# Plain float32 products for the first four head pairs, and weight groups spread over the steps of y

## The chip, the cores and the metric

The kernel runs on one core of a Trainium2 chip. The metric is the device time of one execution in microseconds, as the median of several runs; a profiled execution has its own time, which is given beside it. The core has five engines with a queue each: PE (TensorE, the matrix unit; its weight loads are listed as PEld), DVE (VectorE), ACT (ScalarE), POOL (GpSimd) and SP (SyncE, which here issues the DMAs). Each queue runs in order.

## The reference

Attention over 4 batches of 8 heads, 576 tokens of 64 numbers each, with a second, linear path through a memory; then two feed-forward layers over 2,304 tokens. The inputs are float32, or float64 words for some weights, and the result is wanted at nearly float32 precision.

```python
scores = scale * q @ k.T                 # causal, per head, 576 x 576
a = softmax(scores);  local = a @ v
q_p = where(q > 0, q, exp(q) - 1) + 1
mem_out = (q_p @ M_prev) / (q_p . z_prev + 1e-6)
attn = g * mem_out + (1 - g) * local     # g = sigmoid(beta), per head
x = attn as 2304 x 512
h = x @ w_in                             # 512 -> 2048
y = (s * relu(h)**2 + b) @ w_out         # 2048 -> 512
gate = sigmoid(y @ w_gate);  val = y @ w_val      # 512 -> 1536
out = (gate * val) @ w_out2              # 1536 -> 512
```

## The kernel before

**Products in parts.** PE multiplies operands of type float32r, a rounded float32, at one column after the other. To keep the precision an operand is split into a high part (the value rounded to float32r) and a low part (what is left, float32r again), and a product is made of three: high x high, low x high, high x low. The high part is usually a copy on ACT, the low part a subtraction on DVE or POOL. Weights come as 64-bit words and are first converted to float32 on ACT (L247) and DVE (L250, L253, L259); then ACT (L265) and POOL (L268) split them.

**Stages.** (1) Attention works on 16 jobs j, each a pair of heads of one batch, four to a batch. q, k and v are loaded (SP), q and k are transposed on PE (L413) and split; scores (L623, L649), maximum (DVE, L603), exponent (ACT, L665), scaling by the reciprocal sums (POOL, L681). The rows of P are transposed on PE in eight groups A0 to D1 (L750, GROUPS, 25 blocks of 128 x 128), copied as the high part by ACT (L773) and subtracted for the low part by DVE (L777). v is split on POOL (L587, L590) into 64 high and 64 low columns side by side, M_prev too (L401, L404), and phi(q), transposed, is split into FS by L421, L422 (ACT) and L426, L427 (DVE). `pv(win, e)` (L779) then makes, for head e and each of two windows of tokens (0 to 256, 256 to 576), one accumulator `acc` of 128 rows, the upper 64 for the products with high columns of v, the lower 64 for those with the low ones; every term over P takes two products (L803, L804), the term over M_prev one (L807). ACT copies the lower half into XB (L827) and DVE adds the upper half (L831).

(2) When a batch is done, x is split (ACT L888, POOL L892) and h = x @ w_in is made in 128 chunks of 12 products (L316) that run between the attention of the later batches; ACT applies relu and SP stores r.

(3) y runs in 96 steps, six token windows of 384 by 16 blocks of rows. A step loads r (`rr`), squares it (ACT L1025), scales it (DVE L1029), copies the high part `gh` (ACT L1035), subtracts for the low part `gl` (POOL L1040) and makes 12 products (PE L1054). In the same phase the 24 pieces of w_gate and w_val are converted, combined pair by pair into 12 groups (`plan_blocks`, sums in L1159) and stored in DRAM.

(4) z makes three pairs of token windows. For each pair, 12 groups of products (L1291) from the stored weight groups, added up by DVE (L1303), passed through a sigmoid or multiplied (POOL L1313) to `p`; then six out tiles, each of three groups of four blocks (`plan_out`): copy (ACT L1369), subtraction (DVE L1376), 12 products (L1387).

**Order.** No engine's order is written by hand. Every piece of work is a task with an engine, an assumed duration, an urgency (base plus offset from the dict TUNE), tiles read and written, and buffers taken. `Plan.order` simulates the engines, each time starting the ready task with the lowest urgency, and the instructions are emitted in the order found; semaphores follow from the tiles that instructions share, not from the plan. Buffers of a kind are handed out in the order in which the tasks are listed.

Of the kernel before, what the change touches and what calls it, by code (L numbers as in the profile page):

```python
# [30 lines left out]
}  # L31
ENG = {"split": "POOL"}
RR = 4
RAW2 = 4
RING = 5
SETS = 3


class Plan:
# [25 lines left out]
    def order(self):  # L65
# [34 lines left out]
        while len(out) < len(tasks):  # L100
            for eng in clock:
                if clock[eng] > now:
                    continue
                for n in ready.get(eng, []):
# [15 lines left out]
                    heapq.heappush(events, (end, n))  # L120
                    heapq.heappush(events, (clock[eng], -1))
# [6 lines left out]
            while events and events[0][0] <= now:  # L128
                _, n = heapq.heappop(events)
                if n < 0:  # L130
                    continue
                for x in tasks[n][5]:
                    touches[x] -= 1
                    if not touches[x] and x in self.made:
                        free[self.made[x][0]] += 1
                for m in users[n]:
                    waiting[m] -= 1
# [10 lines left out]
def attention_moe_kernel(  # L148
# [267 lines left out]
    def bank(nt):  # L416
        return "s" if nt <= 4 else "w"
# [6 lines left out]
    def stack_lo(t, ds):  # L424
# [10 lines left out]
        "raw2": RAW2, "f2": FB, "w2": 16, "rr": RR, "gh": 3, "gl": 3, "yacc": 2,  # L435
# [30 lines left out]
    def plan_prep(j):  # L466
# [90 lines left out]

        def f_hi():
# [14 lines left out]
            new=[(bank(nt), ("ft", j)), ("FS", ("FS", j, 0)), ("FS", ("FS", j, 1))], late=250)  # L573
        add(
# [18 lines left out]

        add("POOL", 950, lambda: prep_m(j), u + AT["m"], reads=[("mem", j)], new=[("mst", ("m", j))])
# [928 lines left out]
```

## Time and profile before

| | us |
|---|---|
| runs | 1143.1, 1136.14, 1135.06 (median 1136.14) |
| profiled execution | 1142.42 |
| its span, first to last instruction | 1140.6 |
| PE busy | 1056.0 (93%) |
| DVE busy | 786.0 (69%) |
| ACT busy | 647.3 (57%) |
| POOL busy | 619.2 (54%) |

The mean granted TensorE clock of the span is 0.975 of full speed. A busy PE is not a PE at its peak: products overlap, so a product's listed duration is longer than the distance to the next one's start. An engine that is idle off the chain that ends last costs nothing. The stages follow each other in time: attention alone to about 105 us, attention and h to about 405, h and y to about 507, y to about 706, z and out to the end.

### The profile page before, as it was taken

Reading aid. Unit: us, or ns where it says so; the run is one execution under the profiler, and the core shown is the slowest. Engines: PE = TensorE matmul, PEld = TensorE weight load, DVE = VectorE, ACT = ScalarE, POOL = GpSimd, SP = SyncE. Lnnn points to the kernel's source line nnn. Section 1 sums busy time; section 2 is a strip of 40 time slices with the busy share of each in tenths; the row PEclk is TensorE's granted clock in tenths of the full one; section 3 lists DMA queues with packets and bytes.
Section 4 is the critical chain, followed back from the end, with each engine's and each line's share of the span. In section 5 each row is a group of like instructions: output and inputs, shape, how many; then the busy total and the mean of one; then the engine's idle time right before and its main releaser. Section 6 shows DMA issues by size and latency. Waiting matters only on the chain.

```text
span 1140.6 us, 18761 instructions
## 1 busy us (share of the span) xinstructions
PE 1056.0 (93%) x6496; PEld 986.6 (86%) x6496; DVE 786.0 (69%) x1426; ACT 647.3 (57%) x1407; POOL 619.2 (54%) x598
## 2 busy tenths in 40 slices
PE   4776999999999989988789999999799998999998
PEld 3665999899999989988688999998689997899986
DVE  5999888777677527868999433999826667166631
ACT  4877777777777655545656544555425553245421
POOL 5657566744454335733665653999615775157710
PEclk9989899999999999988899999999999999999999
DMA  5333453333232157649588634545114330043100
GB/s 129 76 78 100 120 158 119 85 94 94 83 95 66 59 185 207 197 139 346 184 250 289 218 112 133 205 156 193 59 44 146 130 129 10 37 138 130 66 19 37
DMA packets 135598, 145.93 MB, mean 128 GB/s; under 512 B 68176, under 2 KB 123472, under 8 KB 135504
## 3 DMA queue, kind: packets, MB, share of 16 engines
q1 hardware_dynamic: 135504, 144.74, 40.5%
q8 instruction: 51, 0.84, 0.3%
q14 instruction: 43, 0.35, 0.1%
HBM read 106.96 MB, written 37.75 MB: 127 GB/s over the span
## 4 chain that ended last, share of the span: by engine, by line
PE 71%; DVE 15%; DMA 4%; issue 3%; POOL 3%; ACT 3%; SPq 0%; ACTq 0%; DVEq 0%; POOLq 0%
PE m L1291 19%; PE h L316 15%; PE o L1387 13%; PE y L1054 11%; PE sc L623 3%; PE acc L803 2%; PE acc L804 2%; DMA rr<-relu_scratch 1%; DVE wm L1159 1%; PE pt_B L750 1%; DVE rr L1029 1%; PE sc L649 1%; PE ft L413 1%; POOL p L1313 1%; DVE yt L1190 1%
## 5 line engine op out<-in xcount | busy, mean ns | idle before, releaser
L1291 PE MATMUL m<-yt,ws 128*128 128x384 f32 x1512 | 266.9, 336 | 6.5 <-POOL ws L1275 3.9
L1291 PEld LDWEIGHTS m<-yt,ws 128*128 128x128 f32 x1512 | 263.6, 189 | 9.1 <-POOL ws L1275 4.8
L316 PE MATMUL h<-x,w_in 128*128 128x256 f32 (+1 forms) x1536 | 233.6, 305 | 6.9 <-ACT r L326 6.9
L316 PEld LDWEIGHTS h<-x,w_in 128*128 128x128 f32 x1536 | 214.3, 194 | 13.1 <-ACT r L326 8.2
L1303 DVE TENSOR_TENSOR set<-m,set 128x384 f32<-128x384 f32 x252 | 134.2, 553 | 57.4 <-PE m L1291 55.3
L1275 POOL TENSOR_TENSOR ws<-wf,ws 128x512 fp32r<-128x512 f32 (+1 forms) x108 | 123.8, 1165 | 90.5 <-ACT ws L1267 90.4
L1054 PE MATMUL y<-gh,w_out 128*128 128x384 f32 x768 | 155.9, 344 | 17.8 <-ACT gh L1035 16.4
L1040 POOL TENSOR_TENSOR gl<-rr,gh 128x384 fp32r<-128x384 f32 x96 | 111.2, 1169 | 112.2 <-ACT gh L1035 83.9
L1387 PE MATMUL o<-w_out,ps 128*128 128x512 f32 x648 | 155.6, 401 | 8.8 <-DVE ps L1376 8.8
L1387 PEld LDWEIGHTS o<-w_out,ps 128*128 128x128 f32 x648 | 123.6, 191 | 39.7 <-DVE ps L1376 10.0
L1054 PEld LDWEIGHTS y<-gh,w_out 128*128 128x128 f32 x768 | 137.6, 193 | 22.4 <-ACT gh L1035 18.8
L1267 ACT CAST ws<-wf 128x512 fp32r<-128x512 f32 (+1 forms) x144 | 81.1, 568 | 94.2 <-PE m L1291 66.7
L1029 DVE TENSOR_SCALAR rr<-rr,sb_s,sb_b 128x384 f32<-128x384 f32 x96 | 62.5, 663 | 71.5 <-ACT rr L1025 69.2
L1313 POOL TENSOR_TENSOR p<-set,set 128x384 f32<-128x384 f32 x72 | 85.2, 1206 | 45.4 <-DVE set L1303 45.4
L681 POOL TENSOR_SCALAR P<-P,rs 128x384 f32<-128x384 f32 (+3 forms) x144 | 82.9, 599 | 42.0 <-DVE rs L673 24.2
L603 DVE CUSTOM_DVE_ANT_0 P<-sc,mask 128x384 f32<-128x384 f32 (+2 forms) x144 | 70.8, 515 | 34.7 <-PE sc L623 19.2
L665 ACT ACTIVATE P<-P,nm 128x384 f32<-128x384 f32 (+2 forms) x144 | 83.8, 583 | 7.4 <-DVE nm L603 6.7
L1054 PE MATMUL y<-gl,w_out 128*128 128x384 f32 x384 | 84.4, 341 | 1.1 <-POOL gl L1040 1.1
L326 ACT ACTIVATE r<-h 128x320 f32<-128x320 f32 (+1 forms) x128 | 52.2, 409 | 57.3 <-PE h L316 42.2
L1376 DVE TENSOR_TENSOR ps<-p,ps 128x512 fp32r<-128x512 f32 x54 | 47.1, 886 | 50.6 <-ACT ps L1369 50.2
L1025 ACT ACTIVATE rr<-rr 128x384 f32<-128x384 f32 x96 | 49.4, 524 | 50.9 <-DMA rr<-relu_scratch 48.8
L1054 PEld LDWEIGHTS y<-gl,w_out 128*128 128x128 f32 x384 | 69.5, 192 | 2.3 <-POOL gl L1040 2.3
(134 smaller groups left out, 1709.8 us busy)
## 6 DMA issues: line engine op xcount, KB each, us to landing
wf<-weight_scratch SPq DMA_DIRECT2D x36, 896.0 KB, 4.6
rr<-relu_scratch SPq DMA_DIRECT2D x96, 192.0 KB, 3.3
raw_w_out<-in_moe_w_out_dram SPq DMA_DIRECT2D x28, 512.0 KB, 4.3
weight_scratch<-wm SPq DMA_DIRECT2D x12, 896.0 KB, 8.0
relu_scratch<-r SPq DMA_DIRECT2D x32, 320.0 KB, 2.3
raw_w_in<-in_moe_w_in_dram SPq DMA_DIRECT2D x16, 512.0 KB, 4.1
relu_scratch<-r SPq DMA_DIRECT2D x32, 256.0 KB, 2.5
raw_gv<-in_moe_w_gate_dram SPq DMA_DIRECT2D x12, 512.0 KB, 5.6
```

Of the source, the lines that this page charges most:

```text
L316: nc.tensor.matmul(t[:, :n], wt[:, wi, c], x[:, xi, c], start=(m == 0), stop=(m == 3 * NK - 1))
L665: nc.scalar.activation(pr, pr, AF.Exp, bias=T.pop(("nm", j, e, t)), scale=-1.0, accum_out=T["sums", j][:, col : col + 1],)
L681: nc.gpsimd.tensor_scalar(out=pr, in0=pr, scalar1=T["rs", j, part][:, n : n + 1], scalar2=1.0, op0=ALU.mult, op1=ALU.mult,)
L1029: nc.vector.tensor_scalar(out=r, in0=r, scalar1=sb_s, scalar2=sb_b, op0=ALU.mult, op1=ALU.add)
L1040: nc.gpsimd.tensor_tensor(out=gl, in0=r_sb.pop(step), in1=gs[step][0].bitcast(F32), op=ALU.subtract)
L1054: nc.tensor.matmul(accs[wi][d][:, :n], w_out_sb[f][:, x, d], y, start=(f == 0 and x == 0 and y is gh), stop=(f == NF - 1 and y is gl),)
L1267: nc.scalar.copy(t[:, 0, :m], flat(a, m))
L1275: engine[LOS[i]].tensor_tensor(out=t[:, 1, :m], in0=flat(a, m), in1=t[:, 0, :m].bitcast(F32), op=ALU.subtract)
L1291: nc.tensor.matmul(acc, wt[:, a, k : k + P], yt[:, y, c], start=(m == 0), stop=(m == 3 * K2 - 1),)
L1303: nc.vector.tensor_tensor(out=t[:, o], in0=Z["m", z, x], in1=t[:, i], op=ALU.add)
L1313: engine[TIMES[o]].tensor_tensor(out=p[:, f + HF * OF[o][0], OF[o][1]], in0=Z["set", z][:, o], in1=Z["set", zg][:, o], op=ALU.mult,)
L1387: nc.tensor.matmul(Z["zo", z], Z["ps", z, i][:, a, k * P : (k + 1) * P], w_out2_sb[f][:, x].rearrange("p c f -> p (c f)"), start=(f == 0 a ...
```

## The change

For the first four jobs (`LEAN`) P, v, M_prev and phi(q) are not split. The transposes of P are copied once, half of the groups on ACT and half on DVE; FS is one copy on DVE; the products take float32 operands as they are, one product a term, into 64 rows; XB is a copy, for e = 0 on ACT and e = 1 on DVE. The splits of v and M_prev on POOL go for these jobs.

In y the scale moves from DVE to POOL and the subtraction for `gl` from POOL to DVE, with more buffers (`RR` 6, `GG` 4). In the plan, the loads for weight group n wait for y step 2 + 7n (`PACE`). The split of x moves from POOL to DVE. The constants are loaded from ACT's queue instead of SP's. A score task takes the buffers of P already (`EARLY`). The three groups of four blocks of an out tile are blocks 0 to 3, 6 to 9, and 4, 5, 10, 11 (`THIRD`), where they were 0 to 3, 4 to 7, 8 to 11. All offsets in TUNE are new; the planner's assumed durations for weight conversion, sums and z's subtractions on DVE are larger; and in its simulation a follower on the same engine is ready when its forerunner leaves the engine.

```diff
-ENG = {"split": "POOL"}
-RR = 4
+ENG = {"split": "DVE"}
+RR = 6
+GG = 4
+PACE = 2, 7
+LEAN = 4
+EARLY = True
...
-        nc.sync.dma_start(gt, beta.partition_broadcast(P))
-        nc.sync.dma_start(sb_s, s_in.partition_broadcast(P))
-        nc.sync.dma_start(sb_b, b_in.partition_broadcast(P))
+        nc.scalar.dma_start(gt, beta.partition_broadcast(P))
+        nc.scalar.dma_start(sb_s, s_in.partition_broadcast(P))
+        nc.scalar.dma_start(sb_b, b_in.partition_broadcast(P))
...
+        def f_copy():
+            T["FS", j] = at.tile([P, NQ * P], F32R, tag="FS0", name=f"FS{j}", bufs=1).bitcast(F32)[:, :n]
+            nc.vector.tensor_copy(T["FS", j], T.pop(("ft", j)))
...
+        if j < LEAN:
+            add("DVE", dve(n), f_copy, w, reads=[("ft", j)], writes=[("FS", j, 0), ("FS", j, 1)])
+            return
...
+        if j < LEAN:
+            return
         add("POOL", 950, lambda: prep_m(j), u + AT["m"], reads=[("mem", j)], new=[("mst", ("m", j))])
...
+        def p_copy(g):
...
+            src, hi, lo = places(g, T.pop(("pt", j, g)))
+            if COPY[g] == "ACT":
+                nc.scalar.copy(hi.bitcast(F32), src)
+            else:
+                nc.vector.tensor_copy(hi.bitcast(F32), src)
...
+            FS = [T["FS", j][i * D : (i + 1) * D] for i in range(2)] if j < LEAN else T["FS", j]
...
+            if j < LEAN:
+                d = slice(e * D, (e + 1) * D)
+                for m, (blk, t, c0, a0, a1) in enumerate(terms):
+                    nc.tensor.matmul(
+                        acc[:D, a0:a1], rawv[:, blk, d],
+                        t[:, 0, c0 : c0 + a1 - a0].bitcast(F32), start=(m == 0), stop=False,
+                    )
+                for m, (f, a0, a1) in enumerate(mem):
+                    nc.tensor.matmul(
+                        acc[:D, a0:a1], T["mraw", j][d, e], f, start=False,
+                        stop=(m == len(mem) - 1),
+                    )
+                return
...
+        def x_copy(win, e):
+            for a, x in parts(win, e):
+                if COPY[win, e] == "ACT":
+                    nc.scalar.copy(x, a[:D])
+                else:
+                    nc.vector.tensor_copy(x, a[:D])
...
         def scale():
             r = r_sb[step]
-            nc.vector.tensor_scalar(
+            nc.gpsimd.tensor_scalar(
                 out=r, in0=r, scalar1=sb_s, scalar2=sb_b, op0=ALU.mult, op1=ALU.add
             )
...
-            nc.gpsimd.tensor_tensor(
+            gl = Y["gp"].tile([P, WT], F32R, tag="gl", name=f"gl{wi}_{f}", bufs=GG)
+            nc.vector.tensor_tensor(
                 out=gl, in0=r_sb.pop(step), in1=gs[step][0].bitcast(F32), op=ALU.subtract
             )
...
-                keys2[i], None, ins=["bar1"], late=True,
+                keys2[i], None, ins=["bar1", ("yc", PACE[0] + PACE[1] * n)], late=True,
...
+    THIRD = [list(range(4)), list(range(HF, HF + 4)), [HF - 2, HF - 1, NF2 - 2, NF2 - 1]]
...
-            ins = [("p", pi)] + [("pp", pi, f, h) for f in range(4 * i, 4 * i + 4)]
+            ins = [("p", pi)] + [("pp", pi, f, h) for f in THIRD[i]]
...
+    COPY = {
+        "A0": "ACT", "A1": "DVE", "B0": "ACT", "B1": "DVE", "B2": "ACT", "C": "DVE", "D0": "ACT",
+        "D1": "DVE", (0, 0): "ACT", (0, 1): "DVE", (1, 0): "ACT", (1, 1): "DVE",
+    }
```

## Rows read from the trace of the kernel before

**Rows 1.** Windows by stage: us, busy time (x instructions) of PE, PEld, DVE, ACT, POOL; clock; DMA

```profile
0.00:120.00 120.00, 81.89 (x506) 65.67 (x507) 98.47 (x234) 81.90 (x194) 75.93 (x97) 0.92 0.39 96
...
120.00:400.00 280.00, 278.36 (x2240) 265.57 (x2240) 206.47 (x508) 211.54 (x527) 144.20 (x181) 1.00 0.34 97
...
512.00:640.00 128.00, 110.48 (x586) 106.84 (x585) 116.81 (x162) 76.09 (x154) 73.08 (x57) 0.93 0.81 272
...
640.00:706.00 66.00, 65.14 (x376) 64.86 (x374) 19.79 (x33) 29.50 (x63) 30.99 (x30) 1.00 0.37 107
...
706.00:820.00 114.00, 102.42 (x540) 96.66 (x541) 107.72 (x144) 62.06 (x117) 96.81 (x72) 0.97 0.47 158
```

**Rows 2.** Chain that ended last, 0 to 125: start, us, what

```profile
43.07 0.61 PE qt L413 x5
...
84.62 0.61 PE qt L413 x5
```

**Rows 3.** Chain, whole span, y phase

```profile
617.24 52.29 PE y L1054 x300
```

**Rows 4.** Window 0 to 118, instructions of line L777 alone

```profile
0.00:118.00 118.00, 17.37 (x32) 0.92 0.38 95
```

**Rows 5.** The same window, line L831 alone

```profile
0.00:118.00 118.00, 7.42 (x20) 0.92 0.38 95
```

**Rows 6.** Lines, 0 to 118: shapes, xcount | busy us, mean ns | idle before

```profile
L426 DVE TENSOR_TENSOR FS<-ft,FS 64x640 fp32r<-64x640 f32 x4 | 3.3, 818 | 0.2
...
L590 POOL TENSOR_TENSOR VHL<-rawv,VHL 128x640 fp32r<-128x640 f32 x6 | 11.0, 1837 | 0.5
```

**Rows 7.** Timeline of PE: start, us, engine, line, op, tiles, xcount

```profile
104.38 0.31 PE L803 MATMUL acc<-PTB,VHL 128*128 128x320 f32 x1
...
104.53 0.31 PE L804 MATMUL acc<-PTB,VHL 128*64 128x320 f32 x1
...
7.38 1.30 PE L413 MATMUL kt<-ident,rawk 128*128 128x128 f32 x5 [7.38 <-DMA rawk<-in_k_dram]
...
319.01 0.71 PE L413 MATMUL kt<-ident,rawk 128*128 128x128 f32 x5
...
402.59 14.07 PE L316 MATMUL h<-x,w_in 128*128 128x320 f32 x108
```

**Rows 8.** Window 120 to 400, line L316 alone

```profile
120.00:400.00 280.00, 161.95 (x1072) 145.08 (x1071) 1.00 0.34 97
```

**Rows 9.** Timeline of SP's queue at the start

```profile
0.74 0.39 SPq L210 DMA_DIRECT2D gt<-in_beta_dram  x1
...
2.12 0.98 SPq L373 DMA_DIRECT2D rawk<-in_k_dram  x2
```

**Rows 10.** Windows of the y phase, line L1054 alone

```profile
512.00:640.00 128.00, 110.48 (x586) 106.84 (x585) 0.93 0.81 272
...
640.00:706.00 66.00, 61.48 (x351) 60.58 (x349) 1.00 0.37 107
```

**Rows 11.** Lines of DVE, 490 to 640

```profile
L253 DVE SCALAR_TENSOR_TENSOR raw_gv<-raw_gv 128x512 int32<-128x512 int32 x24 | 23.3, 971 | 0.8
...
L259 DVE SCALAR_TENSOR_TENSOR raw_gv<-f_gv,raw_gv 128x512 int32<-128x512 int32 x24 | 22.6, 943 | 1.5
...
L250 DVE TENSOR_SCALAR raw_gv<-raw_gv 128x512 int32<-128x512 int32 x24 | 17.6, 735 | 1.5 <-DMA raw_gv<-in_moe_w_gate_dram 1.5
```

**Rows 12.** Single lines: xcount, duration ns min/median/max, first and last start

```profile
L1029 DVE TENSOR_SCALAR rr<-rr,sb_s,sb_b x96: 467/480/1974, 416.4 to 694.8; 128x384 f32<-128x384 f32 x96
...
L1376 DVE TENSOR_TENSOR ps<-p,ps x54: 675/693/2290, 793.5 to 1123.5; 128x512 fp32r<-128x512 f32 x54
```

**Rows 13.** Lines of POOL by shape, whole span

```profile
L681 POOL TENSOR_SCALAR P<-P,rs 128x384 f32<-128x384 f32 x32 | 19.5, 613 | 42.0 <-DVE rs L673 24.2 <-DVE rs L677 9.0 <-PE acc L807 8.8
```

**Rows 14.** Timeline of PE where the out products begin

```profile
810.48 4.86 PE L1387 MATMUL o<-w_out,ps 128*128 128x512 f32 x14 [4.23 <-DVE ps L1376]
...
952.69 7.64 PE L1387 MATMUL o<-w_out,ps 128*128 128x512 f32 x25 [2.87 <-DVE ps L1376]
```

More of the change, by code (lines that the diff above doesn't have):

```diff
@@ L119, in order @@
                         end = max(end, dma + t[7])
-                    heapq.heappush(events, (end, n))
-                    heapq.heappush(events, (clock[eng], -1))
+                    heapq.heappush(events, (end, n, 0))
+                    heapq.heappush(events, (clock[eng], n, 1))
                     break
@@ L128, in order @@
             while events and events[0][0] <= now:
[L129 to L135, printed above, removed]
+                _, n, same = heapq.heappop(events)
+                if not same:
+                    for x in tasks[n][5]:
+                        touches[x] -= 1
+                        if not touches[x] and x in self.made:
+                            free[self.made[x][0]] += 1
                 for m in users[n]:
+                    if (tasks[m][0] == tasks[n][0] and not tasks[n][8]) != bool(same):
+                        continue
                     waiting[m] -= 1
@@ L694, in plan_scores @@
                     reads=[("QT", j), ("KT", j)],
-                    new=[("s", ("sc", j, 0, ts[0])), ("s", ("sc", j, 1, ts[0]))], late=250,
+                    new=[("s", ("sc", j, 0, ts[0])), ("s", ("sc", j, 1, ts[0]))]
+                    + ([(f"P{t}", ("P", j, e, t)) for t in ts for e in range(2)] if EARLY else []),
+                    late=250,
                 )
@@ L699, in plan_scores @@
                     "PE", 6 * mm(S // 2), score_last, w, reads=[("QT", j), ("KT", j)],
-                    new=[("w", ("sc", j, 0, NT4))], late=250,
+                    new=[("w", ("sc", j, 0, NT4))] + ([("P4", ("P", j, 0, NT4))] if EARLY else []),
+                    late=250,
                 )
@@ L707, in plan_scores @@
                     fn = (lambda e=part, t=t: largest(e, t)) if t < NT4 else largest_last
-                    new = [(f"P{t}", ("P", j, part, t))]
+                    new = [] if EARLY else [(f"P{t}", ("P", j, part, t))]
                     if m == part == 0 and t == ts[0]:
                         new.append(("sums", ("sums", j)))
-                    add("DVE", dve(n) + 90, fn, w + part, reads=[("sc", j, part, ts[0])], new=new)
+                    add("DVE", dve(n) + 90, fn, w + part, reads=[("sc", j, part, ts[0])],
+                        new=new, writes=[("P", j, part, t)] if EARLY else [])
                     sums[part].append(("sum", j, part, t))
@@ L941, in plan_weight @@
         add("ACT", 670, scaled, u, reads=[("raw", key)], new=[(fl, ("f", key))])
-        add("DVE", 1500, rest, u, writes=[("raw", key)])
-        add("DVE", 850, joined, u, reads=[("f", key)], writes=[("raw", key)])
+        add("DVE", 1700, rest, u, writes=[("raw", key)])
+        add("DVE", 950, joined, u, reads=[("f", key)], writes=[("raw", key)])
         if tag:
@@ L1068, in plan_step @@
         add("ACT", act(n), square, v, writes=[rk])
-        add("DVE", 450, scale, v, writes=[rk])
+        add("POOL", 700, scale, v, writes=[rk])
         add("ACT", act(n), g_hi, v, reads=[rk], new=[("gh", gk)])
-        add("POOL", 130 + 2.4 * n, g_lo, v, reads=[rk, gk], new=[("gl", ("gl", step))])
+        add("DVE", 650, g_lo, v, reads=[rk, gk], new=[("gl", ("gl", step))])
         new = [("yacc", ("ya", wi))] if f == 0 else []
@@ L1407, in plan_out @@
                 "PE", 12 * mm(512), lambda i=i: out_mm(i), u + i,
-                reads=[k, "bar3b"] + [("w3", f) for f in range(4 * i, 4 * i + 4)],
+                reads=[k, "bar3b"] + [("w3", f) for f in THIRD[i]],
                 writes=[("zo", z)] if i else [], new=[] if i else [("zo", ("zo", z))], late=250,
```

82 lines of the change are left out of this document (54 added, 28 removed), and 12 rows, old and new, of the table TUNE.

## The prediction

> **What bounds the kernel now.** I read the page first (PE is busy 93% of the span, DVE 69%), then the windows by stage, then the chain of waits, then single lines. TensorE is the bound over the whole, so what counts is where PE has nothing to do. In the stretch from 120 to 400 us (attention and h mixed) it is busy 278.36 of 280 us: nothing can be won there but by taking work from PE [rows 1]. It falls short in three places.
>
> First, 0 to 120 us, the first four pairs of heads. No h product can run yet, because h needs x of a whole batch. PE is busy 81.89 us, DVE 98.47 us, at a granted clock of 0.92 [rows 1]; after the start DVE is the fuller engine, and the chain alternates between PE and DVE. A pair takes 20.8 us: two of them lie between the transposes of q at 43.07 and at 84.62 [rows 2].
>
> Second, 512 to 640 us, in y. When nothing is in the way, PE does 300 y products in 52.29 us, 0.174 us each [rows 3]. In this window it does 586 [rows 10], worth 102.1 us, in 128 us: 25.9 us are lost, in waits and at a clock of 0.93. DVE is busy 116.81 of these 128 us, and in the 66 us that follow only 19.79 [rows 1]. Converting the 24 pieces of w_gate and w_val takes 23.3 + 22.6 + 17.6 = 63.5 us of DVE in three lines, all of it before 640 [rows 11]. So DVE is crowded early in y and free late.
>
> Third, the start of z, 706 to 820 us: PE 102.42 and DVE 107.72 of 114 us [rows 1], with 4.23 us of idle PE where the first out products begin and 2.87 us at the second such place, both ended by the subtraction L1376 on DVE [rows 14].
>
> **The change, part by part.** All sums are made against the profiled run, 1142.4 us with its span of 1140.6. The median of the runs shown, 1136.1, is 6.3 us lower; I take the difference off the median.
>
> *Constants loaded from ACT's queue.* On SP's queue the three loads stand ahead of the first load of k: it is issued at 2.12 us instead of 0.74 [rows 9]. It is the head of the chain, so 1.4 us are won. On ACT they pass nothing but the table load; the first work that needs the result is far later.
>
> *Lean pairs, DVE.* L777 (the low parts of P's transposes) takes 17.37 us for four pairs, 4.34 a pair [rows 4]. It goes; of the 25 blocks 11 (A1, B1, C, D1) come back on DVE as plain copies of the same size from PSUM. Saved: 4.34 x 14/25 = 2.43 us. Of the two FS subtractions of 0.818 us [rows 6] one copy of 640 columns stays: saved 0.82. L831 takes 7.42 us for four pairs [rows 5], 1.86 each, and only the half that belongs to e = 1 stays on DVE: saved 0.93. Together 4.2 us a pair. ACT loses about as much, and POOL loses the split of v (1.84 us for its subtraction alone [rows 6]); both are off this path and I count them at nothing.
>
> *Lean pairs, PE.* Columns streamed for one pair before: per head (256 + 128) x 2 + 256 in the first window and (3 x 320 + 192 + 64) x 2 + 320 in the second, 3,776; for two heads 7,552. After: 384 + 256 + 1,216 + 320 = 2,176, for two heads 4,352. A rounded product of 320 columns starts 0.15 us after the one before it, 0.46 ns a column [rows 7]: 3.5 us a pair now. No plain float32 product is in the trace. The lower bound is that same 0.46 ns: 2.0 us a pair, a gain of 1.5. The nearest float32 rows are transposes of 5 x 128 columns: 0.71 us in the dense part, 1.11 ns a column, and 1.30 us at the start, 2.03 ns a column [rows 7]. So 4.8 or 8.8 us a pair. I take 8.8: these products run in that first stage, and a product of full float32 should not be cheaper than a transpose that only moves the numbers. PE then gets 5.3 us more a pair. The Trainium skill (FP8 and Floating Point Precision, TensorE Precision Notes) counts four passes through the array for true FP32; by that, as an estimate, 4 x 0.46 = 1.84 ns a column, 8.0 us a pair, and the sum would be 3 us better for four pairs if PE decides. No run here shows it yet.
>
> *What a lean pair then takes.* DVE: 20.8 - 4.2 = 16.6 us. PE: from 120 to 400 us twelve pairs and 1,072 h products were done [rows 8]; h products come at 14.07/108 = 0.130 us [rows 7], 139.7 us, so a pair is (278.4 - 139.7)/12 = 11.6 us of dense PE, and 16.9 with the 5.3. Two engines that are nearly equal wait for each other; I add 0.9 us, which is a choice, and get 17.8: 3.0 us less a pair, 12 us for four. Bounds: 4.2 x 4 = 17 if DVE alone decides, 0 if PE takes its place. From then on PE is full as before, so what the first h product wins, the end wins.
>
> *Split of x on DVE instead of POOL, EARLY, RR, GG, the planner's costs and offsets.* They change the order and depth of queues. Where PE is full (120 to 400 us) they can win nothing; DVE has 73 us to spare there [rows 1]. I count them at nothing in attention; what the new order brings by chance elsewhere I bound by 4.2 us either way, the longer of the two gaps before out products [rows 14].
>
> *y: scale to POOL, subtraction gl to DVE.* In 512 to 706 us DVE has 116.8 + 19.8 = 136.6 us of work in 194 [rows 1]. The 937 y products there [rows 10] are some 78 steps. Scale costs 0.480 us alone and up to 1.97 [rows 12]; gl on DVE, two SBUF tensors of 384 columns, is bounded below by 0.693 x 384/512 = 0.52 us (L1376, median) and above by 2.29, that line's longest [rows 12]. I take 0.69, near what scale takes with its waits, so DVE's load goes to about 140 us. POOL's scale is near 0.613 us, the same form at the same size in L681 [rows 13].
>
> *y: PACE.* Weight group n may be planned only behind step 2 + 7n. No tile is shared between that product and that load, so I expect no new semaphore on the chip: what changes is the order in SP's queue and in DVE's. Behind a load that stands too early on SP wait the loads of r; with RR 6 they are asked for six steps, 12 us, ahead, and that covers it. If that cover went, PE would wait for a landing, 5.3 us for the first load of k (issued at 2.12, PE starts at 7.38 [rows 7, 9]), at each of twelve groups: 63 us. Spread evenly, DVE's 140 us lie beside 937 x 0.174 + 5 for the first z products = 168 us of PE, 83%. That would free all of the 25.9 us; queues in fixed order never interleave perfectly, so I take 18. Bounds 0 and 25.9.
>
> *z: THIRD.* The second group of four blocks for the out products no longer needs the last two weight groups, so twelve more products stand ready where PE now idles. The two gaps are 7.1 us [rows 14]; I take 3, since DVE is full there with converting w_out2.
>
> Sum: 1.4 + 12 + 18 + 3 = 34.4 us; 1136.1 - 34.4 = 1101.7, say 1102.
>
> **Rivals.** *PE takes DVE's place in the lean pairs.* For: 16.9 against 16.6 us is no margin, and 20.8 us is reached when float32 costs (20.8 - 8.1)/4,352 = 2.9 ns a column. Against: a denser PE should get the full clock. Then 1102 + 12 = 1114.
>
> *DVE stays the bound in y.* gl would wait for POOL's scale each time: 78 x 0.613 = 48 us, DVE 188 of 194, and nothing is won: 1102 + 18 = 1120. The trace speaks for it in that lines of DVE with two SBUF tensors stretch (L1376 from 0.675 to 2.29 us), against it in that the one-tensor scale stretches as well (0.467 to 1.97) [rows 12], so that it may be an even exchange. [...]
>
> *Both.* The change then does hardly what it says: 1132.
>
> *Slower.* One mechanism: gl is last of four operations through three engines (square, scale, gh, gl), and DVE runs in order, so a late gl holds the weight conversions and all behind it. The time is over 1% longer when the stall is over 1.05 us a step: 140 + 78 x 1.05 = 222 us for this part of y, 28 more than now, against 16.4 won elsewhere. At 1.3 us a step it is 241, 47 more: 1136.1 + 47 - 16.4 = 1167.
>
> *Everything is won*: 1.4 + 17 + 25.9 + 7.1 = 51: 1085.
>
> **How the numbers follow.** My forecast 0.46 (own range 1086 to 1118), PE in DVE's place 0.14, y unchanged 0.16, both 0.10, everything 0.07, slower 0.07. About 1% is what a measurement of this kernel can tell from no change. Faster by over 1% is below 1124.8: 0.46 + 0.14 + 0.07 and two thirds of 0.16, 0.78. Within 1%: the rest of that and 0.10, 0.15. Slower: 0.07. The range 1084 to 1133 takes in all but the slower case and the tails.
>
> **What would show it.** In the profile after: the first k load issued near 0.7 us; two transposes of q in the lean pairs about 36 us apart instead of 41.6; lean products' starts some 0.65 us apart for 320 columns (below 0.4 or above 0.9 breaks the PE step); the dense part of PE beginning some 13 us earlier; DVE's share between 640 and 706 us well above a third, with y products on PE 0.174 us apart nearly throughout; the two gaps before out products shorter. The prediction is wrong if PE, not DVE, is full in the first 100 us and the pair still takes 20 us, or if DVE's lines in y stretch so that PE still waits for gh or gl.

## The result, and the profile after

The changed kernel takes 1101.73 us (median of four runs, 1100.46 to 1103.49) against 1137.25 us for the kernel before in the same comparison: a ratio of 0.968, 95% interval [0.964, 0.972]. The prediction was 1102 us. The total came out; the parts it was made of did not, and they are what the rest of this text is about. Of the kernels tried below, those given with a range were run four or five times, the others once.

To compare stages between kernels I cut the span into five pieces. *Attention net* is the start of the last `acc` product less 0.1313 us for each h product done by then (0.130 us in [rows 7]). *h* is 1,536 products x 0.1313 = 201.7 us and *y* 1,152 products x 0.1743 [rows 3] = 200.8 us, both the same for all. *Loss in y* is what the stretch from there to the start of the last y product holds beyond its h, y and early z products. *z* is the rest, the early z products added. The five add up to the span.

| kernel | attention net | loss in y | z | span | profiled execution |
|---|---|---|---|---|---|
| before | 255.7 | 42.3 | 440.1 | 1140.6 | 1142.42 |
| after | 264.2 | 8.3 | 426.8 | 1101.7 | 1103.49 |
| difference | +8.5 | -34.0 | -13.3 | -38.9 | -38.9 |

How far these pieces vary by themselves can be read from kernels below whose engines get the same instructions in the same order all through attention: 264.2, 264.6, 263.1 and 262.9 us of attention net in the changed kernel and three kernels that differ from it only in y, 255.7 and 256.4 in the kernel before and one that differs only in y. Differences of less than 2 us are not read.

So the first stage, from which 13.4 us were to be won, got longer. y gave nearly twice the 18 us expected, z four times its 3 us.

The windows by stage of the kernel after (stretch; us; busy time and instructions of PE, PEld, DVE, ACT, POOL; granted clock; DMA share; GB/s) answer to [rows 1]:

```profile
0.00:120.00 120.00, 89.39 (x480) 60.61 (x480) 78.11 (x208) 66.57 (x159) 56.83 (x78) 0.86 0.36 92
...
512.00:640.00 128.00, 127.02 (x733) 126.70 (x732) 99.78 (x161) 82.31 (x171) 78.71 (x65) 1.00 0.72 238
640.00:706.00 66.00, 64.49 (x372) 64.17 (x371) 42.94 (x72) 36.03 (x72) 37.20 (x33) 1.00 0.66 230
```

From 0 to 120 us DVE is now busy 78.11 us instead of 98.47, and PE gets through 480 matmul records instead of 506 (a lean product shows as two records), at a clock of 0.86 instead of 0.92. PE is now the fuller engine of the two, with 89.39 us, but neither is full, so something else holds the lean pairs. From 512 to 640 us PE does 733 products instead of 586 and idles 1 us of 128: y is dense. In the last row z has already begun; y's last product is at 674.9 us instead of 704.7.

The chain of waits of the kernel after, 36 to 126 us (start, us, what), answers to [rows 2]:

```profile
66.13 0.70 PE qt L419 x5
...
74.08 3.40 DMA zbc<-in_z_prev_dram
77.55 1.54 POOL phit L536
79.11 0.83 DVE nrm L544
...
81.87 1.33 PE ft L419 x5
...
92.69 0.70 PE qt L419 x5
...
98.52 3.58 DMA zbc<-in_z_prev_dram
102.17 1.54 POOL phit L536
...
118.62 0.71 PE qt L419 x5
```

Two lean pairs take 118.62 - 66.13 = 52.5 us, 26.2 a pair, where they took 20.8. And each time the chain passes through something that was no part of it before: the load of z_prev, which is issued only after the last products of the pair ahead (on PE's timeline they end at 68.20 and 94.75 us). The waits of that stretch (20 to 122 us: who waited for what; us, times, longest) say the same:

```profile
POOL phit L536 <- DMA zbc<-in_z_prev_dram: 16.7, 3, 7.6
```

Before, the loads for the same two pairs were issued at 38.45 and 58.11 us, some 15 us ahead of their use at 53.66 and 74.02. SP's queue after, around the first of the two (start, us):

```profile
68.71 1.64 SPq L236 DMA_DIRECT2D raw_w_in<-in_moe_w_in_dram  x2
70.44 1.01 SPq L379 DMA_DIRECT2D rawv<-in_v_dram  x2
...
72.34 1.67 SPq L400 DMA_DIRECT2D mraw<-in_M_prev_dram  x2
74.08 0.58 SPq L402 DMA_DIRECT2D zbc<-in_z_prev_dram  x1
```

The load of z_prev stands behind those of v and M_prev, and these behind a load of w_in for which the queue has waited 5.8 us on POOL (L274). So not every microsecond of the delay is a tile still in use: part of it is the place that the plan gave these loads.

In y, whole span, by lines (shape, count; busy us, mean ns; idle before, by what), the rows that answer to [rows 11] and [rows 12]:

```profile
L1099 POOL TENSOR_SCALAR rr<-rr,sb_s,sb_b 128x384 f32<-128x384 f32 x96 | 105.3, 1104 | 79.5 <-ACT rr L1095 71.9
L1110 DVE TENSOR_TENSOR gl<-rr,gh 128x384 fp32r<-128x384 f32 x96 | 67.2, 702 | 48.8 <-PE y L1124 38.2
...
L259 DVE SCALAR_TENSOR_TENSOR raw_gv<-raw_gv 128x512 int32<-128x512 int32 x24 | 17.8, 741 | 0.8
L265 DVE SCALAR_TENSOR_TENSOR raw_gv<-f_gv,raw_gv 128x512 int32<-128x512 int32 x24 | 16.4, 684 | 0.0
L256 DVE TENSOR_SCALAR raw_gv<-raw_gv 128x512 int32<-128x512 int32 x24 | 11.0, 457 | 0.4 <-DMA raw_gv<-in_moe_w_gate_dram 0.3
```

gl takes 0.70 us on DVE, as predicted (0.69). The scale takes 1.10 us on POOL, not 0.61. And gl now idles before it mostly for PE's y products: its buffers are full ahead of PE, which is what one wants to see. The conversions of w_gate and w_val take 45.2 us of DVE instead of 63.5.

In z the PE timeline has one gap where out products begin (start, us, line, tiles, count, idle before), answering to [rows 14]:

```profile
775.98 46.38 PE L1464 MATMUL o<-w_out,ps 128*128 128x512 f32 x191 [2.05 <-DVE ps L1454]
```

Before there were three (1.66, 4.23 and 2.87 us, 8.8 in all).

### The profile page after: what moved, and what is told of

It reads as the page before. It is cut to its first block, busy times and chain, and to the rows that moved or that the text cites. A ratio compares the mean times of both kernels' runs of the same rounds, so it can differ in the third digit from the quotient of the medians.

```text
span 1101.7 us, 18731 instructions
## 1 busy us (share of the span) xinstructions
PE 1054.2 (96%) x6516; PEld 976.4 (89%) x6516; DVE 752.0 (68%) x1406; ACT 630.1 (57%) x1371; POOL 583.3 (53%) x574
## 4 chain that ended last, share of the span: by engine, by line
PE 80%; POOL 9%; DVE 4%; issue 2%; DMA 2%; ACT 1%; SPq 1%; POOLq 0%; DVEq 0%; ACTq 0%
PE m L1361 17%; PE h L322 17%; PE y L1124 16%; PE o L1464 13%; POOL ws L1345 3%; PE sc L638 3%; POOL p L1383 2%; PE acc L836 2%; PE acc L849 2%; PE pt_B L769 2%; PE acc L850 2%; POOL w_out L274 1%; POOL rr L1099 1%; PE ft L419 1%; PE sc L664 1%
## 5 line engine op out<-in xcount | busy, mean ns | idle before, releaser
L322 PE MATMUL h<-x,w_in 128*128 128x256 f32 (+1 forms) x1536 | 223.0, 301 | 5.4 <-ACT r L332 4.4
L322 PEld LDWEIGHTS h<-x,w_in 128*128 128x128 f32 x1536 | 208.5, 191 | 9.7 <-ACT r L332 5.3
L1124 PE MATMUL y<-gh,w_out 128*128 128x384 f32 x768 | 148.7, 334 | 1.0 <-ACT gh L1105 1.0
L1099 POOL TENSOR_SCALAR rr<-rr,sb_s,sb_b 128x384 f32<-128x384 f32 x96 | 105.3, 1104 | 79.5 <-ACT rr L1095 71.9
L1124 PEld LDWEIGHTS y<-gh,w_out 128*128 128x128 f32 x768 | 134.3, 188 | 1.3 <-ACT gh L1105 1.3
L696 POOL TENSOR_SCALAR P<-P,rs 128x384 f32<-128x384 f32 (+4 forms) x144 | 87.8, 631 | 67.0 <-DVE rs L692 35.4
L1110 DVE TENSOR_TENSOR gl<-rr,gh 128x384 fp32r<-128x384 f32 x96 | 67.2, 702 | 48.8 <-PE y L1124 38.2
L680 ACT ACTIVATE P<-P,nm 128x384 f32<-128x384 f32 (+3 forms) x144 | 83.2, 579 | 29.3 <-DVE nm L618 28.8
L332 ACT ACTIVATE r<-h 128x320 f32<-128x320 f32 (+1 forms) x128 | 52.5, 411 | 62.8 <-PE h L322 54.9
L618 DVE CUSTOM_DVE_ANT_0 P<-sc,mask 128x512 f32<-128x512 f32 (+4 forms) x144 | 69.2, 513 | 23.1 <-PE sc L638 17.4
L1105 ACT CAST gh<-rr 128x384 fp32r<-128x384 f32 x96 | 49.0, 511 | 46.2 <-PE y L1124 41.1
```

The lines of the kernel that those rows point to most:

```text
L322: nc.tensor.matmul(t[:, :n], wt[:, wi, c], x[:, xi, c], start=(m == 0), stop=(m == 3 * NK - 1))
L618: nc.vector.tensor_tensor_reduce(out=pr, in0=ps, in1=mk, scale=1.0, scalar=3e38, op0=ALU.add, op1=ALU.min, accum_out=nm,)
L680: nc.scalar.activation(pr, pr, AF.Exp, bias=T.pop(("nm", j, e, t)), scale=-1.0, accum_out=T["sums", j][:, col : col + 1],)
L696: nc.gpsimd.tensor_scalar(out=pr, in0=pr, scalar1=T["rs", j, part][:, n : n + 1], scalar2=1.0, op0=ALU.mult, op1=ALU.mult,)
L1099: nc.gpsimd.tensor_scalar(out=r, in0=r, scalar1=sb_s, scalar2=sb_b, op0=ALU.mult, op1=ALU.add)
L1124: nc.tensor.matmul(accs[wi][d][:, :n], w_out_sb[f][:, x, d], y, start=(f == 0 and x == 0 and y is gh), stop=(f == NF - 1 and y is gl),)
```

## The experiments

### What a plain float32 product costs

A kernel of its own: five blocks of 48 products of 320 columns, float32r and float32, with 128 or 64 stationary columns or 64 rows; the rest of the computation is left out.

> Leaves the whole computation out: five series of 48 products of 320 columns, one after the other, with nothing else on PE: float32r with 128 and with 64 stationary columns, plain float32 with 64 and with 128, and plain float32 with 64 rows. If true float32 costs four passes, 0.53 to 0.60 us from start to start in all three float32 series against 0.13 to 0.15 for float32r. If the lean products of the changed kernel show the price rightly (six in 1.83 us, 0.28 us each), 0.26 to 0.30 with 64 columns; with 128 columns the same if the number of passes is what counts, double if a narrow stationary operand shares the array.

PE's lines of that kernel (count | busy us, mean ns | idle):

```profile
L30 PE MATMUL acc<-raw 128*64 128x320 f32 x96 | 27.9, 453 | 3.4 <-DMA raw<-in_q_dram 3.4
L32 PE MATMUL acc<-raw 128*128 128x320 f32 x96 | 26.1, 433 | 0.0
L34 PE MATMUL acc<-raw 64*64 64x320 f32 x96 | 26.1, 430 | 0.0
L26 PE MATMUL acc<-rnd 128*128 128x320 f32 x48 | 7.5, 315 | 0.0
L28 PE MATMUL acc<-rnd 128*64 128x320 f32 x48 | 7.2, 309 | 0.0
```

48 float32r products take 7.5 us, 0.156 us each, 0.49 ns a column. 48 plain float32 products stand in the trace as 96 records and take 26.1 us: 0.272 us a record, 0.543 a product, 1.70 ns a column. The block with 64 stationary columns (L30) has 27.9 us because six of its records ran first of all and took 3.46; its other 90 take 24.44 us, 0.272 each again, so neither the width of the stationary operand nor the number of rows makes a difference. 0.543 us a product is in the range of the four passes; the second range of the expectation ("0.28 us each") had taken a record for a product. In the changed kernel three lean products of 320 columns show as six records from 59.82 us on, and the next shape starts at 61.49: 0.278 us a record. So a lean pair's products take 4,352 x 1.70 = 7.4 us; 8.8 had been taken, from a transpose.

The ratio, 3.5, is near the four passes that the Trainium skill gives for true FP32 (FP8 and Floating Point Precision, TensorE Precision Notes): 8.0 us a pair had been the estimate by it, and the trace agrees with it better than with the row that was taken, a transpose at the start.

### The lean pairs

**Taken out of the changed kernel.**

```diff
-LEAN = 4
+LEAN = 0
```

> The changed kernel with LEAN = 0: no pair is lean, all the rest of the change stands, and the plan is made anew. Theory A (the lean products hold the buffers of v and M_prev, so the lean pairs cost time): the first h product and the dense part of PE come 6 to 12 us earlier than the 124 us of the changed kernel, and the time is 1090 to 1096. Rival B (the lean pairs win the 12 us that the prediction gave them, and something else in attention lost them): the dense part comes later than 130 us and the time is 1110 to 1116.

1108.62 us (1107.65 to 1109.71; ratio to before 0.972, [0.970, 0.974]), 6.9 us more than the changed kernel. Attention net 268.9. The time lies between the two ranges: the first h product comes earlier, at 115.2 us instead of 122.6, as theory A had it, and yet the time is longer. So the lean pairs win 4.7 us where they stand, and the new order without them is 13.2 us longer than before. y and z are as in the changed kernel (9.1 and 427.2).

**The early claim alone, and with lean pairs, in the kernel before.** The diff is of the first kernel; the second has `LEAN = 4`.

```diff
+LEAN = 0
+EARLY = True
...
+                    + ([(f"P{t}", ("P", j, e, t)) for t in ts for e in range(2)] if EARLY else []),
```

> The kernel before with one part of the change: a score task takes the buffers of P already (EARLY). With no pair lean the attention of the changed kernel cost 13 us more than before, net of the h products done in it (268.9 against 255.7). Theory A: it is EARLY that costs them, because scores wait for buffers of P: attention, net of h, 262 to 270 us, and 1144 to 1152 in all. Rival B: the new offsets do, and EARLY does nothing: 254 to 258 net, 1135 to 1142.

> The kernel before with EARLY and with the first four pairs lean; offsets, y and z as before. If the lean pairs win as much here as in the changed kernel (268.9 - 264.2 = 4.7 us), attention net of h is 4 to 6 us under that of EARLY alone. If they win the 12 us of the prediction once the offsets are the old ones, 10 to 14 under it. If the held buffers of v and M_prev cost more than the lean pairs save, it is above it.

1145.28 us and 1154.62 us, against 1140.02 for the kernel before in the same comparison. The first total alone says little, since runs of the kernel before reach 1145.23; attention net, 261.4 and 269.8, says more, and y and z are unchanged within 3 us (39.7 and 439.9; 41.5 and 439.0). The early claim costs 5.7 us, and on top of it, in the old order, the lean pairs cost 8.4 us more. An edit that by the prediction's sum takes 4.2 us of DVE's work off each pair made the kernel slower: loads of engines alone don't explain it.

**What holds them: the loads.** Lean products read `rawv` and `mraw` as loaded. Before, POOL split v and M_prev into tiles of their own early in the pair, and the raw tiles, one buffer each, were free for the next load; now they are held until the pair's last product, and the load of z_prev stands behind that of M_prev on SP's queue. The test gives them two buffers.

```diff
-        raw = T["mraw", j] = at.tile([P, 2, D], F32, tag="mraw", name=f"mraw{j}", bufs=1)
+        raw = T["mraw", j] = at.tile([P, 2, D], F32, tag="mraw", name=f"mraw{j}", bufs=2)
-        z = T["z", j] = at.tile([P, 2, D], F32, tag="zbc", name=f"zbc{j}", bufs=1)
+        z = T["z", j] = at.tile([P, 2, D], F32, tag="zbc", name=f"zbc{j}", bufs=2)
...
-        "s": 4, "w": 1, "h": 2, "r": 2, "rawq": 1, "rawk": 1, "rawv": 1, "mem": 1, "mst": 2,
+        "s": 4, "w": 1, "h": 2, "r": 2, "rawq": 1, "rawk": 1, "rawv": 1, "mem": 2, "mst": 2,
```

> The changed kernel with two buffers each for the loaded v and for M_prev with z_prev, on the chip and in the plan; LEAN stays 4. Theory A: the loads of the next pair no longer wait for the last product of this one; the distance of two transposes of q falls from 26.6 us a pair to 17 to 19, the dense part of PE begins at 98 to 106 us, and the time is 1075 to 1085. Rival C (a lean pair is slow because of its products on PE at a low clock): the distance stays above 25 us and the time at 1100 to 1104.

> Two buffers for M_prev and z_prev alone; v keeps one. If the wait of the memory path for z_prev is what costs (POOL waits 16.7 us for that load in three pairs), most is won: dense part at 104 to 112 us, 1082 to 1090. If v is held just as long, less than half of what two buffers for both win: 1094 to 1102.

The first of the two doubled the tile for v as well; it does not compute the reference's result, so its 1097.95 us (1096.08 to 1099.27) is only a sign of direction, and what a second tile for v is worth stays open. The second, with v's tile left single, took 1094.4 us: attention net 257.0, 7.2 us less than in the changed kernel, y and z nearly the same (7.7, 425.4). The wait of `phit` for the load of z_prev, 16.7 us in the changed kernel, is no longer among the nine longest of that stretch. This is at the lower edge of the second range, not in the first: the wait is gone, but only part of what it measured was won. The planner knows of the buffers too, so the 7.2 us are those of the buffers and of the order that it made with them.

**Lean pairs alone, not held, in the old order.** The kernel before with `LEAN = 4` and the same two buffers; no early claim, old offsets, constants still on SP.

> The kernel before with the lean pairs alone, in the old order (the tiles of P not claimed ahead of the scores), and with two buffers instead of one for M_prev and for z_prev, so that the next pair's loads needn't wait for the last product of this pair. Engines, buffers and offsets of y and z as before. The attention's end less its h products was 255.7 us in the kernel before, 269.8 us with the lean pairs and the early claim in the old order, 261.4 us with the early claim alone. Theory A, lean pairs are worth the 12 us that were predicted once their operands' buffers don't hold up the next loads: 241 to 247 us, and a time of 1126 to 1133 us. Theory B, the float32 products give back most of what VectorE saves, as they did in the new order (4.7 us won with held buffers): 249 to 254 us, time 1133 to 1139 us. Theory C, they win nothing at all here: 256 us or more, 1140 us or more.

1132.76 us; attention net 245.7, 10.0 us less than before, y and z as before (42.7 and 440.1). That is inside the first theory's ranges: the 12 us predicted for the lean pairs are there to within 2 us, once the operands' buffers don't hold up the loads. No run has the two buffers without lean pairs; in the kernel before `phit` waits for z_prev once in the first 125 us, 3.9 us for the first pair, and POOL's split never for M_prev, so that there is little for the buffers to win alone. Its first 120 us, in the form of the windows above:

```profile
0.00:120.00 120.00, 97.97 (x576) 68.70 (x577) 90.65 (x230) 76.55 (x181) 70.26 (x89) 0.97 0.43 110
```

PE has 576 matmul records here (506 before, 480 in the changed kernel) at a clock of 0.97 (0.92 and 0.86). The transposes of q of the third to the sixth pair on PE's timeline:

```profile
40.68 0.77 PE L418 MATMUL qt<-ident,rawq 128*128 128x128 f32 x5
68.41 0.77 PE L418 MATMUL qt<-ident,rawq 128*128 128x128 f32 x5
88.11 0.77 PE L418 MATMUL qt<-ident,rawq 128*128 128x128 f32 x5
103.55 0.77 PE L418 MATMUL qt<-ident,rawq 128*128 128x128 f32 x5
```

The sixth is at 103.55 us, where it was at 110.48 before, and the third at 40.68 instead of 42.91: 21.0 us a pair on the mean where it was 22.5, in uneven steps of 27.7, 19.7 and 15.4. The predicted 17.8 us a pair is not what is seen, and the first h product is even later than before (109.3 against 105.5 us). What was won is attention work of the later pairs done sooner, as these rows read, not an earlier h.

**The old order in the changed kernel.** The two buffers, the old offsets of attention, h and w_in, no early claim, split of x back on POOL; the planner's rule and costs, y and z as changed. The dict's line is cut short here.

```diff
-    "lq": -552.7, "lk": -837.4, "lv": -423.9, "lm": 221.4, "q": -226.8, "k": -35.1, "phi": 30.4,
...
+TUNE = {'lq': -464.0, 'lk': -691.2, 'lv': -261.0, 'lm': 480.1, 'q': -140.1, 'k': -66.1, 'phi': 44.5, ...
...
-ENG = {"split": "DVE"}
+ENG = {"split": "POOL"}
-EARLY = True
+EARLY = False
```

> The changed kernel with two buffers for M_prev and z_prev, and with its attention put back into the old order: the old offsets of the attention (y's and z's stay new), no early claim of P's tiles, split of x on GpSimd. Theory A, the new order of the attention costs what the runs so far leave unexplained (268.9 us net without lean pairs against 255.7 before): the attention ends at 241 to 250 us net against 257.0 with the two buffers in the new order, and the time is 1080 to 1089 us. Theory B, the order is indifferent or fits the lean pairs, and something else holds the attention: 255 to 260 us net, 1092 to 1098 us.

1087.79 us (1087.35 to 1088.23; ratio to before 0.955, [0.950, 0.960]), attention net 248.2, y 8.1, z 426.8. The first theory holds. This is 14 us faster than the changed kernel and 53 us faster than the one before. Between the two profiled executions the difference is 16.0 us, all of it in attention: 7.2 us by the buffers and 8.8 by the order. Which of the three parts of the order carries the 8.8 was not separated further; the early claim cost 5.7 when it was alone.

### y

**Without the pacing.** The wait of weight group n for step 2 + 7n is taken out of the plan.

```diff
-                keys2[i], None, ins=["bar1", ("yc", PACE[0] + PACE[1] * n)], late=True,
+                keys2[i], None, ins=["bar1"], late=True,
```

> The changed kernel without PACE: the loads for the weight groups wait for no step of y in the plan. In y PE lost some 42 us before and 8 after, net of its h and y products. Theory A: spreading the groups is what won them: the loss is back at 25 us or more, the time at 1118 to 1135. Rival B (offsets and buffers of the new plan keep DVE free for y anyway): the loss stays under 15 us, 1100 to 1108.

1102.86 us, loss in y 7.3 us. The line of the pacing, to which the prediction gave y's gain, does nothing that one run can show. But the run does not test the spreading itself. The first line of each conversion (count, shortest, median and longest ns, first and last start) in the kernel before, the changed kernel, and this one:

```profile
L250 DVE TENSOR_SCALAR raw_gv<-raw_gv x24: 418/422/2064, 489.6 to 619.7; 128x512 int32<-128x512 int32 x24
L256 DVE TENSOR_SCALAR raw_gv<-raw_gv x24: 414/422/740, 483.5 to 650.9; 128x512 int32<-128x512 int32 x24
L256 DVE TENSOR_SCALAR raw_gv<-raw_gv x24: 414/419/425, 481.1 to 625.1; 128x512 int32<-128x512 int32 x24
```

Counted in steps of y done by then, the conversions run from step 15 to 57 before, from 4 to 84 in the changed kernel, and still from 3 to 72 without the pacing: the rest of the new plan spreads them nearly as far by itself. Whether y would be as dense without that spread, no run shows.

**Scale and gl back on their engines.**

```diff
-            nc.gpsimd.tensor_scalar(
+            nc.vector.tensor_scalar(
...
-            nc.vector.tensor_tensor(
+            nc.gpsimd.tensor_tensor(
```

> The changed kernel with scale on DVE and the subtraction gl on POOL again, in code and in plan; PACE stays. If the exchange of engines did its part of the 34 us in y, the loss of PE in y is 15 to 30 us and the time 1108 to 1124. If it was an even exchange, as the prediction counted it, the loss stays at 5 to 12 us and the time at 1098 to 1106.

1110.66 us, loss in y 16.6 us: the exchange is worth 8.3 us in this one run, and is not even. DVE's lines in this kernel:

```profile
L265 DVE SCALAR_TENSOR_TENSOR raw_gv<-f_gv,raw_gv 128x512 int32<-128x512 int32 x24 | 25.1, 1045 | 1.4
L259 DVE SCALAR_TENSOR_TENSOR raw_gv<-raw_gv 128x512 int32<-128x512 int32 x24 | 21.8, 908 | 0.8
L256 DVE TENSOR_SCALAR raw_gv<-raw_gv 128x512 int32<-128x512 int32 x24 | 17.0, 706 | 12.1 <-DMA raw_gv<-in_moe_w_gate_dram 9.0 <-DMA raw_gv<-in_moe_w_val_dram 3.0
```

With gl on POOL the three conversion lines cost DVE 63.9 us again, with scale there 45.2. Two places on the timeline show how. In the kernel before (start, us, engine, line), POOL and then DVE:

```profile
430.42 1.02 POOL L1040 TENSOR_TENSOR gl<-rr,gh 128x384 fp32r<-128x384 f32 x1 [1.58 <-PE y L1054]
...
430.56 1.09 DVE L1029 TENSOR_SCALAR rr<-rr,sb_s,sb_b 128x384 f32<-128x384 f32 x1 [1.51 <-ACT rr L1025]
431.57 0.42 DVE L250 TENSOR_SCALAR raw_w_out<-raw_w_out 128x512 int32<-128x512 int32 x1
...
444.62 1.14 POOL L1040 TENSOR_TENSOR gl<-rr,gh 128x384 fp32r<-128x384 f32 x1
...
444.81 1.24 DVE L250 TENSOR_SCALAR raw_w_out<-raw_w_out 128x512 int32<-128x512 int32 x1
```

L250 takes 0.42 us by itself and 1.24 when it is issued 0.19 us into a gl on POOL: it is done about 0.3 us after gl is. L1029, 0.47 at its shortest [rows 12], takes 1.09 in the same position. DVE waits gl out. In the changed kernel POOL can be the one that waits (rows of DVE and POOL, in order of time):

```profile
513.91 0.56 DVE L1110 TENSOR_TENSOR gl<-rr,gh 128x384 fp32r<-128x384 f32 x1 [0.45 <-PE y L1124]
...
514.24 1.29 POOL L1099 TENSOR_SCALAR rr<-rr,sb_s,sb_b 128x384 f32<-128x384 f32 x1 [3.13 <-ACT rr L1095]
...
514.39 0.69 DVE L265 SCALAR_TENSOR_TENSOR raw_gv<-f_gv,raw_gv 128x512 int32<-128x512 int32 x1
...
608.27 0.67 POOL L1099 TENSOR_SCALAR rr<-rr,sb_s,sb_b 128x384 f32<-128x384 f32 x1 [1.92 <-ACT rr L1095]
...
608.38 1.02 DVE L1160 COPY yf<-y 128x384 f32<-128x384 f32 x2
```

Beside copies out of PSUM the scale takes 0.67 us. At 514.24 it is issued 0.33 us into a gl on DVE, with L265 right behind; both read two tensors of SBUF and keep their time (0.56 and 0.69), and the scale takes 1.29 and ends 0.45 us after L265. The Trainium skill (SBUF, State Buffer, Who interferes with whom) has this as an exclusive lock on a pair of ports that VectorE and GpSimd share; whoever issues first has it for the whole instruction and the other blocks, and both a two-input instruction and a `tensor_scalar` in its two-port form contend for it. The trace agrees in these rows: the one that is issued into the other's run waits it out, and L265, issued while the scale stood waiting, keeps its time. The rival had VectorE pay for the move. Over the whole of y GpSimd pays most, with 1.10 us a scale, and has room for it (78.71 of 128 us busy from 512 to 640); VectorE's three lines fall to 45.2 us, though not to their shortest (L259 takes 0.74 on the mean and 0.69 at its shortest).

**Short rings.** The changed kernel with 4 buffers for r and 3 each for gh and gl.

```diff
-RR = 6
-GG = 4
+RR = 4
+GG = 3
```

> The changed kernel with the buffers of y back at their old number: 4 for r instead of 6, 3 each for gh and gl instead of 4. All else is unchanged, the engines of scale and gl and the offsets included. The earlier runs put 8 us of the 34 us won in y on the exchange of engines and none on the pacing; this asks for the rest. Theory A, the depth won it (a load of r or a conversion that comes late no longer stops TensorE): y loses 25 to 40 us to waiting again instead of 8, and the time is 1118 to 1135 us. Theory B, it is the order in which the weight groups and steps are queued (the offsets): y still loses at most 15 us and the time is 1102 to 1110 us.

1122.07 us. Loss in y 21.9 us instead of 8.3, and z 432.7 instead of 426.8: the loss lies between the two theories' ranges, the time in the first one's, and the depth is worth 13.6 us in y. PE's timeline shows what the short rings let through:

```profile
547.87 0.97 PE L1124 MATMUL y<-gl,w_out 128*128 128x384 f32 x4 [0.97 <-DVE gl L1110]
554.23 1.78 PE L1124 MATMUL y<-gh,w_out 128*128 128x384 f32 x8 [3.28 <-ACT gh L1105]
557.40 1.65 PE L1124 MATMUL y<-gl,w_out 128*128 128x384 f32 x4 [1.39 <-DVE gl L1110]
```

Five and a half of PE's idle microseconds stand in these three places alone; in the changed kernel PE idles 1 us in all between 512 and 640, since gl and gh lie ready.

**Rings and exchange alone, in the kernel before.**

```diff
-RR = 4
+RR = 6
+GG = 4
...
-            nc.vector.tensor_scalar(
+            nc.gpsimd.tensor_scalar(
...
-            nc.gpsimd.tensor_tensor(
+            nc.vector.tensor_tensor(
```

> The kernel before with two things of y alone: the deeper buffers (6 for r, 4 each for gh and gl) and the exchange of engines (scale on GpSimd, gl on VectorE) with the costs that the planner takes for these two. Attention, offsets, pacing, the other costs and the order of z stay as they were before. Taken out of the changed kernel, the buffers cost 15 us of waiting in y and the exchange 8, of 34 won. Theory A, the two are the whole of it: y loses at most 12 us instead of 42 (less the z products done early), time 1103 to 1110 us. Theory B, they are worth here what they were worth there, and the rest is in the order in which y's loads and steps are queued: y loses 15 to 25 us, time 1112 to 1124 us. Theory C, they only work together with the new order of y: y loses 30 us or more, time 1128 to 1140 us.

1115.99 us (1114.57 to 1122.2; ratio to before 0.977, [0.974, 0.980]). The profiled run (1122.2) is the longest of the five, 6.2 us over their median, so its pieces may be too long by that much. In it attention net is 256.4, z 440.2, the loss in y 21.3 us: 21.0 won of the changed kernel's 34.0, close to the 13.6 + 8.3 that the two were worth when taken out. The second theory holds. The chain of that kernel shows what is left:

```profile
575.07 4.12 DMA rr<-relu_scratch
...
586.06 8.87 DMA rr<-relu_scratch
...
597.62 6.75 DMA rr<-relu_scratch
...
609.22 9.62 DMA rr<-relu_scratch
...
638.88 6.47 DMA rr<-relu_scratch
```

Loads of r, 4 to 10 us long on the chain, between 575 and 650 us. In the changed kernel the loads of r make 1.6% of the chain from 400 to 690 us, one of them, at 447.28, nearly all of it. There the remaining 13 us go with the rest of the change to y, the new order (the offsets of y, the planner's costs and its rule for followers on one engine; the line of the pacing is not needed for it); which of these, no run separates. A wider spread of the conversions may be part of it: here they run from step 15 to 72.

## Why the prediction was right, and where it was wrong

**The total** was right by luck, because two errors nearly cancelled: attention was 22 us worse than summed (8.5 lost for 13.4 won), y and z 26 us better (47.3 won for 21).

**Constants on ACT: right.** The first load of k is issued at 0.74 us and its transpose starts at 6.24 us instead of 7.38 [rows 7]: 1.1 us, 1.4 predicted. What the end gains by it was not tried alone.

**Lean pairs: the size is nearly there, the way to it is not.** The price of float32 products was 1.70 ns a column and not 2.03, 3.9 us more of PE a pair instead of 5.3, and the lean pairs with two buffers win 10.0 us where 12 were summed. But a pair takes 21.0 us there, not 17.8, and "what the first h product wins, the end wins" fails both ways: with two buffers in the old order h starts 3.8 us later and 10.0 us are won, without lean pairs in the new order it starts 7.4 us earlier and 4.7 are lost. In the changed kernel the step that failed is the sentence on POOL: it "loses the split of v", and that was counted at nothing because POOL is off the path. The splits of v and of M_prev, which the sentence doesn't name, were also what freed the raw tiles. Of a removed instruction only its duration was counted, not the tile that it released. For M_prev, with the load of z_prev behind it, that costs 7.2 us; for v it stays open.

**Order, EARLY, split of x "at nothing in attention": wrong.** Without lean pairs the new order is 13.2 us longer than the old one, 5.7 of it by the early claim when that is alone. The bound of 4.2 us either way had been taken from gaps in z; the stage that these edits touch is the first, where PE is not full. The prediction named 120 to 400 us as the stretch in which they can win nothing, which holds for the changed kernel (278.64 of 280), and overlooked that they can lose in the one before it.

**"A denser PE should get the full clock": not borne out for the first 120 us.** PE was busy 81.89 us of them at a mean clock of 0.92 before, 89.39 at 0.86 after, and 97.97 at 0.97 in the lean pairs with two buffers. The kernel with rings and exchange alone has the same instructions there as the kernel before:

```profile
0.00:120.00 120.00, 86.12 (x504) 69.99 (x505) 98.23 (x234) 81.85 (x194) 76.36 (x96) 0.79 0.38 95
```

It got 0.79, and its attention net is 0.7 us longer. So the mean clock of this stretch follows neither the kernel nor how busy PE is, and between these two kernels it decided little.

**y: the mechanism was wrong.** The 18 us were given to the pacing, whose line is worth nothing in the changed kernel (whether the spread that the rest of the plan makes is worth anything stays open), and the deeper rings were given nothing of their own, only the part of covering late loads of r, though they are worth about 14 us in y and 6 in z when taken out of the changed kernel (in the kernel before, where they came with the exchange, z is 440.2 us as without them). The exchange was called even; it is worth 8. The upper bound, 25.9 us, covered 512 to 640 us only; of the 42.3 us some 16 more were lost before, where PE is busy 46.3 us of each 50 from 400 to 500. The price of the scale on POOL, 0.61 us, was that of a row in a stage where DVE runs other work; it is 1.10.

**The rival that ended slower**, PE held by a late gl, was the right place to look but had the wrong sign: gl has more buffers, and waits for PE (38.2 us) instead of being waited for.

**z: the size was off.** PE's idle time in z fell from 15.3 us (6.5 before its m products, 8.8 before the out products) to 6.4 (4.3 and 2.1): 8.9 us of the 13.3; part of the rest goes with the granted clock, 0.97 in the first 115 us of z before and 0.99 after. The waits before the out products closed by 6.7 us, near the prediction's bound of 7.1, which it had halved because DVE was full. Whether the new groups of blocks did it or z's new offsets was not tried.

## What to carry to other kernels

An instruction that is removed has a duration and a set of tiles that it sets free: when operands are read where they were loaded, ask what the next load of that tile now waits for, and give it a second buffer before judging the idea. Where a stage is short of PE work by waits spread over several engines, look first whether the rings between them are full ahead of PE (then the producers wait for PE) or empty (then PE waits for them), and try deeper ones before reordering. And a total that comes out right says nothing of its terms: only taking the parts out one by one showed that 14 us were being lost in this change.

## What the runs showed of the hardware

A plain float32 product appears as two matmul records, 0.272 us each for 320 columns, 1.70 ns a column together, 3.5 times a float32r product; neither 64 instead of 128 stationary columns nor 64 instead of 128 rows makes it cheaper. And of a VectorE and a GpSimd instruction that meet, either may pay, in the rows shown the one that was issued into an instruction already at work: a one-tensor VectorE instruction of 0.42 us took 1.24 when issued 0.19 us into a GpSimd subtraction, and a GpSimd scale of 0.67 us took 1.29 when issued 0.33 us into a two-tensor VectorE instruction with another behind it.
